# Pairwise sums of the q*k products for half of chunk 2, a norm on unscaled row sums, and a new order of all steps in a one-core transformer block

## The chip, the cores and the metric

The kernel runs on one core of one Trainium2 chip. The metric is the device time of one execution in microseconds, the median of several runs. A shorter time is better.

## What is computed

One block of a transformer on 2048 rows of 512 values in bf16: a layer norm, attention over a short dilated window, a residual sum, a second layer norm, a gated feed-forward network, and a second residual sum. Cut to what matters:

```python
H = 32; Dh = D // H; W, dil = 8, 2            # 32 heads of 16, 8 keys two rows apart
idx = pos[:, None] - arange(W) * dil           # keys s, s-2, ..., s-14
logits = einsum("bhsd,bhswd->bhsw", q, kg) * Dh ** -0.5
attn = softmax(where(mask, logits, -1e9))
o = einsum("bhsw,bhswd->bhsd", attn, vg)
h = x + o @ wo                                 # qkv = layernorm(x) @ wqkv
g = layernorm(h) @ W_gate; u = layernorm(h) @ W_up     # F = 1376
out = h + ((g * (g > 0)) * u) @ W_down
```

## The kernel before

The rows are cut into four chunks of 512 rows (0 to 3), each of four blocks of 128. Each chunk goes through the same stages.

*First norm* (`layernorm` without `residual`): statistics on VectorE (line 469), normalization on ScalarE or VectorE (lines 514, 517), transposed on TensorE (line 546) or, for chunk 3, by DMA on SP (line 535).

*q, k, v* (line 587): 12 groups of 4 matmuls of 512 columns into a PSUM bank, copied out by ScalarE (line 595). In chunk 0 the first groups are cut into pieces that wait for single slices of the weights and single blocks of x.

*Scores*: the window's 8 offsets are done in two halves of 4. For a half, VectorE multiplies q with the shifted k in two instructions of 4096 elements a partition (line 638; chunk 0 in pieces of 2048, line 653), each for two of the four channel groups. TensorE then sums over channels with a selector matrix (line 644): 16 matmuls a half, each 32 columns wide, four side by side. For the two halves of chunk 3 the tuple `PRE` makes it otherwise: VectorE first adds the two products (line 682), and 8 matmuls are left (line 689).

*Softmax and values*: exponentials on ScalarE (line 703); the sum over the window (lines 735, 720), its reciprocal (726, 729), the scaling (747); the weights are spread over partitions by DMAs on SP (line 763); VectorE multiplies with v (lines 795, 810), and the 8 products are added by an accumulating DMA from POOL (line 838) and two VectorE steps (lines 798, 832, in chunk 0 also 802).

*Output projection and residual* (line 876): TensorE, then line 887 on VectorE adds x and keeps the row sum in `sm`.

*Second norm* (`layernorm` with `residual`): line 452 scales each row sum by -1/D into `mv`, line 458 on ScalarE sums the squares of x minus mean, line 512 on VectorE subtracts the mean. The division by the deviation is left to the end of the feed-forward network, as a factor of 1/variance (lines 479, 486). The rows are transposed on TensorE for chunk 0 and by four DMAs on SP for chunks 1 to 3 (line 535).

*Feed-forward*: gate and up (line 949; the last 96 columns line 916), ScalarE copies them out (953, 956), VectorE multiplies them (977, tail 926), the tail is transposed by a DMA on SP (935), and the down projection (line 1000) follows in two parts, 8 of the 11 groups and then 3. The end is added on ScalarE and a POOL DMA (chunks 0 and 1) or on VectorE (line 1008, chunks 2 and 3), then stored.

**What sets the order.** Every step is an `Op` in a plan. The table `RANK` gives a number for each step, and `Plan.order` takes the steps in that order, works out a start for each from the durations that are written beside the steps (`MM`, `D40` and so on, and the times at which loads are expected, `XT` and `WT`), and issues them sorted by that start. On the chip each engine then runs its own list in order, with waits where data is needed. So a change of `RANK` or of a duration can move any step against any other, on every engine and on the DMA queues of SP and POOL. Buffers are shared: 8 PSUM banks, 6 big tiles of 4096 elements, two tiles each for the gate and up results.

Of the kernel before, what the change touches and what calls it, by code (L numbers as in the profile page):

```python
# [8 lines left out]
P = 128  # L9
BF16 = mybir.dt.bfloat16  # L10
F32 = mybir.dt.float32
I32 = mybir.dt.int32
ACT = mybir.ActivationFunctionType
# [80 lines left out]
class Plan:  # L94
# [21 lines left out]
    def order(self):  # L116
        self.flight = [8.65, 9.0, 9.4, 11.5, 12.9, 14.9, 16.2, 19.6]
        waiting = sorted(self.ops, key=lambda o: (o.prio, o.seq), reverse=True) if RANK else list(self.ops)
        free = {}
# [82 lines left out]
def kernel(  # L202
# [20 lines left out]
    PADL = 16  # L223
    DEN1 = (0, 1, 2, 3)
    BCD = {(0,0):"SSSS",(0,1):"SSSS",(1,0):"SSSS",(1,1):"SSSS",(2,0):"SSSS",(2,1):"SSSS",(3,0):"SSSS",(3,1):"SSSS"}
    PRE = ((3,0),(3,1))
    PRD = ()
    ODA = (0, 1)
    LATE = "ud"
# [860 lines left out]
```

## Time and profile before

| | us |
|---|---|
| median of 3 runs (lowest, highest) | 192.83 (192.31, 192.97) |
| the profiled execution | 193.22 |
| its span, first to last instruction | 191.3 |
| TensorE matmuls busy | 185.3 (97%) |
| VectorE busy | 149.6 (78%) |
| ScalarE busy | 115.2 (60%) |
| GpSimd busy | 18.5 (10%) |

The profile calls TensorE's matmuls PE and its weight loads PEld, VectorE DVE, ScalarE ACT and GpSimd POOL; a q behind an engine's name is the list of DMAs that it issues. Rows of the timeline and of the chain of waits begin with the start and the length in microseconds; in brackets stands how long the engine was idle before and what ended that. Groups give the count, the busy time and the mean length of one in ns. A VectorE instruction's length is more than the distance to the next one, since neighbours overlap a little, so a run of equal instructions gives the step. The granted TensorE clock was 0.997 over the span.

### The profile page before, as it was taken

What the parts mean: (1) busy time and instruction counts of PE and PEld (TensorE: products, weight loads), DVE (VectorE), ACT (ScalarE), POOL (GpSimd) and SP (SyncE); (2) the same over time, 40 slices, a digit from 0 to 9 for tenths busy, and PEclk for the clock granted to TensorE, in tenths of its full rate; (3) what the DMA queues carried; (4) which work ended last, traced back from release to release, by engine and by line L of the source; (5) the groups of instructions that cost most, each with busy time, mean ns of one, the idle gap of its engine ahead of it and who ended that gap; (6) DMA issues with size and microseconds to landing.
All of it is one profiled execution on the core that took longest, in us unless ns stands there. A gap on an engine that the chain in (4) does not pass through costs nothing.

```text
span 191.3 us, 3033 instructions
## 1 busy us (share of the span) xinstructions
PE 185.3 (97%) x1101; PEld 96.5 (50%) x1120; DVE 149.6 (78%) x246; ACT 115.2 (60%) x236; POOL 18.5 (10%) x34
## 2 busy tenths in 40 slices
PE   7899999999999999999999999999999999999993
PEld 7795555544455444644445544444446444445452
DVE  6899999999999999999999987999627503212632
ACT  2589999976748967753454875144855528517500
POOL 3000002500000042000055000042100000000000
PEclk9999999999999999999999999999999999999998
DMA  5998464992068589993479916779900460120302
GB/s 159 331 351 327 102 157 84 200 196 45 0 258 228 168 154 193 183 279 61 88 131 186 203 33 139 164 151 186 211 4 0 82 165 0 31 82 0 82 25 88
DMA packets 26718, 26.44 MB, mean 138 GB/s; under 512 B 12528, under 2 KB 22608, under 8 KB 26704
## 3 DMA queue, kind: packets, MB, share of 16 engines
q1 hardware_dynamic: 23248, 16.39, 30.9%
q0 software_dynamic: 2736, 8.91, 25.1%
q10 hardware_dynamic: 720, 0.95, 1.5%
q8 instruction: 9, 0.15, 0.3%
q14 instruction: 5, 0.04, 0.1%
HBM read 8.42 MB, written 2.10 MB: 55 GB/s over the span
## 4 chain that ended last, share of the span: by engine, by line
PE 94%; DMA 3%; issue 1%; ACTq 0%; DVE 0%
PE bank L949 36%; PE bank L587 22%; PE bank L1000 20%; PE bank L876 7%; DMA wqk_sb<-in_A_wqkv_dram 3%; PE bank L644 3%; PE bank L916 3%; PE bank L546 2%; PE bank L689 1%; PE bank L720 0%; ACTq L324 0%; ACTq L322 0%; DVE row L1008 0%
## 5 line engine op out<-in xcount | busy, mean ns | idle before, releaser
L949 PE MATMUL bank<-quad,wgu_sb 128*128 128x512 bf16 x311 | 72.1, 379 | 0.4
L949 PEld LDWEIGHTS <-wgu_sb 128*128 128x128 bf16 x320 | 30.9, 98 | 36.9 <-issue 1.7
L1000 PE MATMUL bank<-wd_sb,gT 128*128 128x512 bf16 (+3 forms) x195 | 39.6, 355 | 0.2
L956 ACT ACTIVATE gr<-bank 128x512 bf16<-128x512 f32 x40 | 23.2, 607 | 17.0 <-PE bank L949 13.0
L977 DVE TENSOR_TENSOR gT<-gr,up_sb 128x1024 bf16<-128x1024 bf16 x20 | 13.7, 688 | 23.5 <-ACT up_sb L953 20.3
L587 PE MATMUL bank<-quad,wqk_sb 128*128 128x512 bf16 (+2 forms) x171 | 30.0, 319 | 1.0 <-DMA wqk_sb<-in_A_wqkv_dram 0.7
L953 ACT CAST up_sb<-bank 128x512 bf16<-128x512 f32 x40 | 22.6, 594 | 10.5 <-PE bank L949 8.5
L1000 PEld LDWEIGHTS <-gT 128*128 128x128 bf16 (+1 forms) x198 | 18.5, 98 | 19.9
L638 DVE TENSOR_TENSOR big<-quad,kT 128x4096 bf16<-128x4096 bf16 x11 | 24.9, 2283 | 0.0
L587 PEld LDWEIGHTS <-wqk_sb 128*128 128x128 bf16 x176 | 16.9, 114 | 11.2 <-DMA wqk_sb<-in_A_wqkv_dram 0.9
L795 DVE TENSOR_TENSOR big<-big,vT 128x4096 bf16<-128x4096 bf16 x9 | 20.2, 2282 | 0.0
L458 ACT ACTIVATE junk<-x_sm,mv 128x512 bf16<-128x512 bf16 x16 | 11.7, 730 | 10.0 <-DVE mv L452 9.9
L587 PE MATMUL bank<-quad,wv_sb 128*128 128x512 bf16 x63 | 15.6, 379 | 0.1
L876 PE MATMUL bank<-wo_sb,quad 128*128 128x512 bf16 x63 | 15.2, 379 | 0.1
L838 POOL DMA_DIRECT2D big<-big x12 | 11.2, 1018 | 38.5 <-PE bank L587 29.4
L887 DVE SCALAR_TENSOR_TENSOR x_sm<-x_sm,bank 128x512 bf16<-128x512 bf16 x16 | 10.5, 680 | 3.7 <-PE bank L876 3.7
L798 DVE TENSOR_TENSOR big<-big 128x1024 bf16<-128x1024 bf16 (+2 forms) x18 | 11.5, 655 | 0.1
L1008 DVE SCALAR_TENSOR_TENSOR row<-bank,iv,x_sm 128x512 bf16<-128x512 f32 (+2 forms) x10 | 6.2, 640 | 6.8 <-PE bank L1000 6.8
L469 DVE BATCH_NORM_STATS2 st<-x_sm 128x6 f32<-128x512 bf16 x16 | 10.3, 681 | 1.2 <-DMA x_sm<-in_A_x_dram 1.2
L595 ACT CAST kT<-bank 128x512 bf16<-128x512 f32 x16 | 9.1, 592 | 2.8 <-DVE big L638 2.8
L595 ACT CAST quad<-bank 128x512 bf16<-128x512 f32 x16 | 9.4, 596 | 2.1 <-PE bank L587 1.9
L595 ACT CAST vT<-bank 128x512 bf16<-128x512 f32 x16 | 9.4, 596 | 2.0 <-PE bank L587 2.0
(79 smaller groups left out, 173.7 us busy)
## 6 DMA issues: line engine op xcount, KB each, us to landing
big<-big POOLq DMA_DIRECT2D x12, 512.0 KB, 5.7
big<-ex SPq DMA_DIRECT2D x32, 128.0 KB, 2.7
wqk_sb<-wqk_sb POOLq DMA_DIRECT2D x3, 512.0 KB, 4.5
wgu_sb<-in_B_W_gate_dram SPq DMA_DIRECT2D x1, 1376.0 KB, 11.2
wgu_sb<-in_B_W_up_dram SPq DMA_DIRECT2D x2, 688.0 KB, 4.7
wd_sb<-in_B_W_down_dram SPq DMA_DIRECT2D x2, 640.0 KB, 5.2
x_sm<-in_A_x_dram SPq DMA_DIRECT2D x2, 512.0 KB, 7.2
x_sm<-up_sb POOLq DMA_DIRECT2D x4, 256.0 KB, 5.1
```

What stands on the lines that cost most here:

```text
L458: nc.scalar.activation(out=junk[:, j % 2, :], in_=h.t[:] if h else x_sm[:, tk * BPC + j, :], func=ACT.Square, bias=mv.t[:, j, 0:1], scale= ...
L587: nc.tensor.matmul(mm.t[:, lo:hi], lhsT=wv_sb[:, dt, t:D:NT] if c == 2 else wqk_sb[:, dt, c * D + t:(c + 1) * D:NT], rhs=xnT.t[:, dt, lo:h ...
L595: nc.scalar.copy(out=o, in_=mm.t[:])
L638: V.tensor_tensor(out=pb.t[:].rearrange("p (t w) s -> p t w s", t=2), in0=q4, in1=k4, op=ALU.mult)
L795: V.tensor_tensor(out=mt.t[:], in0=ab.t[:], in1=v8, op=ALU.mult)
L798: V.tensor_tensor(out=mt.t[:, 0:n, :], in0=mt.t[:, 0:n, :], in1=mt.t[:, n:2 * n, :], op=ALU.add)
L876: nc.tensor.matmul(od.t[:], lhsT=OT.t[:, t, j * P:(j + 1) * P], rhs=wo_sb[:, t, :], start=(t == 0), stop=(t == NT - 1 and tk not in RPE))
L949: nc.tensor.matmul(mm.t[:fs, lo:hi], lhsT=wgu_sb[:, dt, g, ft * P: ft * P + fs], rhs=hnT.t[:, dt, lo:hi], start=(dt == 0), stop=(dt == NT ...
L953: nc.scalar.copy(out=ub.t[:fs, i, :], in_=um.t[:fs, :])
L956: nc.scalar.activation(out=gr.t[:fs, i, :], in_=gm.t[:fs, :], func=ACT.Relu)
L977: V.tensor_tensor(out=gt.t[:fs, 0:n, :], in0=gr.t[:fs, 0:n, :], in1=ub.t[:fs, 0:n, :], op=ALU.mult)
L1000: nc.tensor.matmul(od.t[:, c0:c1], lhsT=gts[ft].t[:fs, ft % 2, j * P:(j + 1) * P], rhs=wd_sb[:fs, ft, c0:c1], start=(ft == 0), stop=(ft == ...
```

## The change

Four things change.

1. `PRE` also holds (2, 1): in half 1 of chunk 2 VectorE adds the two products, and the scores take 8 matmuls instead of 16.
2. The second norm uses the row sums as they are. Line 452 is gone; the squares are taken of (sum - 512 x), the rows are written as 512 x - sum, and the epsilon is scaled by 512 squared. `eps_t` gets a second column, one more memset on POOL in the setup. The factor cancels in the 1/variance at the end.
3. Many durations of the planner are set anew: the expected loads, the DMAs' landing times and when a late transfer is assumed.
4. `RANK` is a new table.

```diff
-    PRE = ((3,0),(3,1))
+    PRE = ((2,1),(3,0),(3,1))
...
-    eps_t = sb.tile([P, 1], F32, name="eps_t")
+    eps_t = sb.tile([P, 2], F32, name="eps_t")
...
-        nc.gpsimd.memset(eps_t[:], EPS)
+        nc.gpsimd.memset(eps_t[:, 0:1], EPS)
+        nc.gpsimd.memset(eps_t[:, 1:2], EPS * D * D)
...
-    XT = (3.1, 3.25, 4.1, 5.9, 7.15, 8.65, 9.0, 9.4, 12.9, 14.85)
+    XT = (3.45, 3.65, 4.05, 5.3, 7.15, 8.65, 9.0, 9.4, 13.0, 14.5)
...
-                    late = 3.0 if at < free.get("DT", -1.0) + 0.8 else 0.0
+                    late = 3.0 if at < free.get("DT", -1.0) - 0.5 else 0.0
...
-                    def f_nm(j=j):
-                        V.tensor_scalar(out=mv.t[:, j, 0:1], in0=sm.t[:, j:j + 1], scalar1=-1.0 / D,
-                                        scalar2=None, op0=ALU.mult)
...
-                                             bias=mv.t[:, j, 0:1], scale=1.0, accum_out=sq.t[:, j:j + 1])
+                                             bias=sm.t[:, j:j + 1], scale=-float(D), accum_out=sq.t[:, j:j + 1])
...
-                    V.tensor_scalar(out=xn.t[:], in0=x, scalar1=mv.t[:, j, 0:1], scalar2=None, op0=ALU.add)
+                    V.tensor_scalar(out=xn.t[:], in0=x, scalar1=float(D), scalar2=sm.t[:, j:j + 1], op0=ALU.mult, op1=ALU.subtract)
```

The new order at three places. First VectorE between the scaling of chunk 1's softmax weights (`ex`, second row of the first piece) and the first multiplication with v. Before:

```order
L747 TENSOR_TENSOR ex_100<-ex_100,rec_103 128x512
L638 TENSOR_TENSOR big_91<-quad_87,kT 128x4096
L638 TENSOR_TENSOR big_89<-quad_87,kT 128x4096
L638 TENSOR_TENSOR big_92<-quad_87,kT 128x4096
L795 TENSOR_TENSOR wqk_sb<-big_88,vT 128x4096
L795 TENSOR_TENSOR big_90<-big_88,vT 128x4096
```

After the change (the lines have moved by a few: 638 is 635, 682 is 679, 795 is 799):

```order
L751 TENSOR_TENSOR ex_100<-ex_100,rec_103 128x512
L635 TENSOR_TENSOR big_92<-quad_87,kT 128x4096
L635 TENSOR_TENSOR big_89<-quad_87,kT 128x4096
L679 TENSOR_TENSOR big_91<-big_91,big_92 128x4096
L635 TENSOR_TENSOR big_90<-quad_87,kT 128x4096
L981 TENSOR_TENSOR gT_93<-gr_111,up_sb_110 128x1024
L799 TENSOR_TENSOR wqk_sb<-big_88,vT 128x4096
```

The sum of chunk 2's two products (L679) and one gate-up product now stand ahead of the multiplications with v of chunk 1.

Second, VectorE at the second norm of chunk 1 (`x_sm,sm_122` are the residual sums with their row sums, `row` the rows to be transposed). Before:

```order
L926 TENSOR_TENSOR row_104<-gr_111,bank_139 128x2x96
L452 TENSOR_SCALAR mv_118<-sm_122 128x1
L512 TENSOR_SCALAR row_107<-x_sm,mv_118 128x512
L926 TENSOR_TENSOR row_104<-gr_111,bank_144 128x2x96
L887 SCALAR_TENSOR_TENSOR x_sm,sm_122<-x_sm,bank_140 128x512
L452 TENSOR_SCALAR mv_118<-sm_122 128x1 x2
L512 TENSOR_SCALAR row_108<-x_sm,mv_118 128x512
L977 TENSOR_TENSOR gT_98<-gr_112,up_sb_110 128x1024
```

After (887 is 891, 512 is 509, 977 is 981):

```order
L891 SCALAR_TENSOR_TENSOR x_sm,sm_122<-x_sm,bank_142 128x512
L981 TENSOR_TENSOR gT_98<-gr_112,up_sb_110 128x1024
L509 TENSOR_SCALAR row_105<-x_sm,sm_122 128x512
L891 SCALAR_TENSOR_TENSOR x_sm,sm_122<-x_sm,bank_143 128x512
L509 TENSOR_SCALAR row_108<-x_sm,sm_122 128x512
L891 SCALAR_TENSOR_TENSOR x_sm,sm_122<-x_sm,bank_139 128x512
L509 TENSOR_SCALAR row_107<-x_sm,sm_122 128x512
```

The scaled row sums (L452) are gone, each residual sum is followed by its subtraction, and the two tail products (L926) have moved far ahead.

Third, SP's list at the same place: the transposes of chunk 1's rows (`quad_81`), of chunk 0's tail products (`gT_97`), and the DMAs that spread chunk 2's softmax weights (from `ex`). Before:

```order
L763 DMA big_88<-ex_102 128x1x512 x4
L535 DMA_TRANSPOSE quad_81<-row_107 128x4x128
L935 DMA_TRANSPOSE gT_97<-row_104 128x4x128
L535 DMA_TRANSPOSE quad_81<-row_105 128x4x128
L535 DMA_TRANSPOSE quad_81<-row_108 128x4x128
L535 DMA_TRANSPOSE quad_81<-row_106 128x4x128
```

After (535 is 532, 935 is 939, 763 is 767):

```order
L939 DMA_TRANSPOSE gT_97<-row_106 128x4x128
L532 DMA_TRANSPOSE quad_81<-row_105 128x4x128
L532 DMA_TRANSPOSE quad_81<-row_108 128x4x128
L532 DMA_TRANSPOSE quad_81<-row_107 128x4x128
L532 DMA_TRANSPOSE quad_81<-row_104 128x4x128
L767 DMA big_88<-ex_102 128x1x512 x4
```

The tail's transpose now stands ahead of the four rows' transposes, and the spreading DMAs stand behind them.

More of the change, by code (lines that the diff above doesn't have):

```diff
@@ L459, in f_sq @@
                                              func=ACT.Square,
-                                             bias=mv.t[:, j, 0:1], scale=1.0, accum_out=sq.t[:, j:j + 1])
-                    a = nms[j] = add((ln + "nm" + gk, tk), "DVE", DSM, f_nm, [src[j][0]], pr, take=[mv], use=[sm], lat=DL)
-                    ag.append(add((ln + "sq" + gk, tk), "ACT", 0.66 if h else 0.72, f_sq, [a], pr,
-                                  take=[sq], use=[mv] + ([h] if h else []), lat=AL))
+                                             bias=sm.t[:, j:j + 1], scale=-float(D), accum_out=sq.t[:, j:j + 1])
+                    ag.append(add((ln + "sq" + gk, tk), "ACT", 0.66 if h else 0.72, f_sq, [src[j][0]], pr,
+                                  take=[sq], use=[sm] + ([h] if h else []), lat=AL))
                 else:
@@ L522, in norm @@
                 f = lambda: f_xn(j, xn)
-                d, u = ([nms[j]], [mv]) if residual else ([e], [nb, rs] if on_act else [mv, rs])
+                d, u = ([src[j][0]], [sm]) if residual else ([e], [nb, rs] if on_act else [mv, rs])
                 if on_act:
                     return xn, add((ln + "xn" + gk, tk), "ACT", AX, f, d, pr, take=[xn], use=u, lat=AL)
-                return xn, add((ln + "xn" + gk, tk), "DVE", DXN, f, d, pr, take=[xn], use=u, lat=DL)
+                return xn, add((ln + "xn" + gk, tk), "DVE", 0.27 if residual else DXN, f, d, pr, take=[xn], use=u, lat=DL)
             step = 1 if tk == 0 and not residual else 2
@@ L684, with f_pb, f_sc @@
                 a = add(("pa%d" % hf, tk), "DVE", D40, f_pa, [a for a, _, _ in prd], apr, use=[b for _, b, _ in prd], lat=DL)
-                def f_sc(sc=sc, pb=prd[0][1]):
-                    for u in range(2):
+                nu = 2
+                if (tk, hf) in PRE2:
+                    def f_pb(p0=prd[0][1]):
+                        V.tensor_tensor(out=p0.t[:, 0:4, :], in0=p0.t[:, 0:4, :], in1=p0.t[:, 4:8, :], op=ALU.add)
+                    a = add(("pb%d" % hf, tk), "DVE", D20, f_pb, [a], apr, use=[prd[0][1]], lat=DL)
+                    nu = 1
+                def f_sc(sc=sc, pb=prd[0][1], nu=nu):
+                    for u in range(nu):
                         for g in range(4):
@@ L894 @@
             else:
-                a = add(("rs%d" % j, tk), "DVE", 0.63, f_rs, [a], base + 50, take=[sm], use=[od], lat=DL)
+                a = add(("rs%d" % j, tk), "DVE", 0.613, f_rs, [a], base + 50, take=[sm], use=[od], lat=DL)
             hd.append((a, od))
```

37 lines of the change are left out of this document (19 added, 18 removed), and 76 rows, old and new, of the table RANK.

## The prediction

> **What bounds the kernel now.** I read the page first: the busy line, two rows of the slices, and the chain of the work that ended last.
>
> ```profile
> span 191.3 us, 3033 instructions
> ...
> PE 185.3 (97%) x1101; PEld 96.5 (50%) x1120; DVE 149.6 (78%) x246; ACT 115.2 (60%) x236; POOL 18.5 (10%) x34
> ...
> PE   7899999999999999999999999999999999999993
> ...
> DVE  6899999999999999999999987999627503212632
> ...
> PE 94%; DMA 3%; issue 1%; ACTq 0%; DVE 0%
> ```
>
> The chain is TensorE for 94%. VectorE is as full as TensorE for the first 24 slices and half empty after them. So there are two questions: what TensorE has to do, and whether VectorE feeds it in time in the first 110 us. A busy TensorE may still wait inside a busy stretch, so I went on to the chain piece by piece (start, length, what) and to TensorE's timeline at its start.
>
> ```profile
> 8.14 0.81 PE L587 MATMUL bank<-quad,wqk_sb 128*128 128x128 bf16 x11 [0.69 <-DMA wqk_sb<-in_A_wqkv_dram]
> ```
> ```profile
> 60.58 0.98 PE bank L644 x16
> ...
> 95.38 0.55 PE bank L689 x8
> ...
> 120.66 7.13 PE bank L1000 x33
> ...
> 188.20 0.35 DVE row L1008
> ```
>
> The last wait of TensorE with a length worth naming ends at 8.14 us, when a slice of the q/k weights lands. From there to 188.2 the chain is one piece of TensorE behind the other: 33 matmuls of 512 columns take 7.13 us, 0.216 each, and the only breaks are the short pieces called issue, 1% of the span in all. So the time is: 8.1 us of loads, 180 us of matmuls without a gap, and a tail of 191.3 - 188.2 = 3.1 us (one VectorE piece of 0.35, then the last store). Whatever is taken from TensorE in those 180 us is gained whole; whatever makes it wait is lost whole, because nothing later can catch it up.
>
> **What the change takes from TensorE.** Half 1 of chunk 2 had 16 score matmuls and now has 8. Both forms stand in the chain above: 16 cost 0.98 us, 8 (chunk 3, which already had them) cost 0.55. That is **-0.43 us**. TensorE has 2242 rows in the order of before and 2226 now, 8 matmuls and their 8 weight loads less, so this is all that TensorE gains.
>
> **What it puts on VectorE.** These rows carry the prices: first the group, then the timeline.
>
> ```profile
> L682 DVE TENSOR_TENSOR big<-big,big 128x4096 bf16<-128x4096 bf16 x1 | 2.3, 2285 | 0.0
> ```
> ```profile
> 7.83 0.79 DVE L517 TENSOR_SCALAR row<-x_sm,mv,rs 128x512 bf16<-128x512 bf16 x2
> ...
> 55.47 0.32 DVE L452 TENSOR_SCALAR mv<-sm 128x1 f32<-128x1 f32 x4
> ...
> 56.05 1.13 DVE L512 TENSOR_SCALAR row<-x_sm,mv 128x512 bf16<-128x512 bf16 x4
> 57.44 6.68 DVE L638 TENSOR_TENSOR big<-quad,kT 128x4096 bf16<-128x4096 bf16 x3
> ...
> 119.45 0.15 DVE L452 TENSOR_SCALAR mv<-sm 128x1 f32<-128x1 f32 x1
> 119.64 0.35 DVE L512 TENSOR_SCALAR row<-x_sm,mv 128x512 bf16<-128x512 bf16 x1
> ```
>
> The new sum of 4096 elements is the 2285 ns instruction. Behind another it starts (6.68 - 2.28) / 2 = **2.20 us** later, so it adds 2.20. The 16 scaled row sums go: four in a row cost 0.08 each, one alone with the wait behind it 0.19 (119.45 to 119.64). That is -1.3 to -3.0 in all; I take 0.09 each, near the row of four, -1.4. The subtraction now has two operations with one value from a tile. Its price is not in the trace. From below stands L512, (1.13 - 0.35) / 3 = 0.26 a step; from above L517, two operations with two values from tiles, 0.79 - 0.40 = 0.39. I take 0.26, the row of the same place and operands, and keep 16 x 0.13 = 2.1 us for the range. VectorE's net is +0.8 us, and between -0.8 and +3.0. The squares on ScalarE keep their count and shape, and no longer wait for a row sum.
>
> All of this lies beside TensorE's work. It costs nothing as long as VectorE's results still come before TensorE wants them. That depends on the new order, so I took the places where TensorE waits for VectorE and counted, for each, what stands ahead of it now and not before, at the steps above and at these: 0.60 for a gate-up product or a 1024-element tree step, 0.27 for the small tail product, 0.34 for a 512-element product, 0.61 for a residual sum. First the margins of before: the last VectorE piece, then the matmuls that need it.
>
> ```profile
> 81.39 0.43 DVE L832 TENSOR_TENSOR quad<-big 128x512 bf16<-128x512 bf16 x1
> ...
> 113.60 1.09 DVE L832 TENSOR_TENSOR quad<-big 128x512 bf16<-128x512 bf16 x3
> ```
> ```profile
> 82.25 3.62 PE L876 MATMUL bank<-wo_sb,quad 128*128 128x512 bf16 x16
> ...
> 115.32 2.75 PE L876 MATMUL bank<-wo_sb,quad 128*128 128x512 bf16 x12
> ```
>
> - Output projection of chunk 0: one 4096 product (2.20) has moved behind it on VectorE, and on TensorE one score group (0.98) and one group of four matmuls (0.86). VectorE has 0.4 more room than before.
> - Output projection of chunk 1: VectorE done at 81.82, TensorE there at 82.25, margin 0.4. Now VectorE has +2.20 + 0.60 + 2 x 0.27 - 4 x 0.09 - 0.34 = +2.6 ahead; TensorE has two down-projection halves of 8 matmuls more and the 8 score matmuls less, 3.46 - 0.43 = +3.0. Margin 0.8.
> - Chunk 2: 114.69 against 115.32, margin 0.6. VectorE +2.20 + 0.60 + 2 x 0.34 - 8 x 0.09 - 0.27 = +2.5, TensorE again +3.0. Margin 1.1.
> - The scores of chunk 2, half 1, which wait for the new sum: VectorE +4.0 ahead, TensorE +5.9. Before, the first product of L638 above was done by 59.7 and the scores began at 60.58: 0.9 then, 2.7 now.
>
> So at these places the new order has more room than the old one, and the searched order has paid for the 2.20 us by moving TensorE's own work forward.
>
> **The one place with less room** is the first gate/up matmul of chunk 1, which needs four transposes on SP, each issued behind a normalized row. Before (SP's own times, the landing times of the four, and TensorE):
>
> ```profile
> 87.23 1.78 SPq L535 DMA_TRANSPOSE quad<-row  x1
> 89.11 1.20 SPq L935 DMA_TRANSPOSE gT<-row  x1
> 90.41 3.87 SPq L535 DMA_TRANSPOSE quad<-row  x3
> ```
> ```profile
> DMA to landing us min/median/max: 2.4/2.5/3.0
> ```
> ```profile
> 95.86 8.81 PE L949 MATMUL bank<-quad,wgu_sb 128*128 128x512 bf16 x39
> ```
>
> Five transposes went one behind the other; the last was issued 1.2 before 94.28, at 93.07, and landed 2.4 later, at 95.5: margin 0.4. Now the first row is ready later by 2.20 + 0.27 + 0.60 - 5 x 0.09 - 0.34 - 2 x 0.61 = 1.06. The transpose of the tail product (L935) has gone ahead of the four, because its product is made some 12 us earlier, and that saves 1.30. TensorE is there 0.43 earlier. Margin 0.4 - 1.06 + 1.30 - 0.43 = 0.2: I count no wait, and this is the tightest place of the new order.
>
> **The start.** The loads are issued as before, but one more memset on POOL stands ahead of the one that guards the last weight slice, and TensorE uses that slice after four matmuls fewer (2 x 0.11 = 0.22 us earlier).
>
> ```profile
> 3.74 0.33 SPq L339 DMA_DIRECT2D wqk_sb<-in_A_wqkv_dram  x1
> ```
> ```profile
> wqk_sb<-in_A_wqkv_dram SPq DMA_DIRECT2D x1, 256.0 KB, 5.7
> ```
>
> It landed at 9.44; TensorE wanted it at about 9.7 and now wants it at 9.5. I put 0.05 for that, between 0 and 0.2. The statistics of the fourth block of x now stand ahead of the second block's normalization, which ties two more steps to that load; in this execution the matmuls of the first two slices, which wait till 8.14 anyway, cover it.
>
> **Sum**: -0.43 + 0.05 = -0.38. The profiled execution took 193.22 us (191.3 and 1.9 around it), so it would take 192.84. The median of the runs shown is 192.83, 0.39 lower; by the same step it comes to **192.45 us**.
>
> [...]
>
> **Rivals.**
> 1. *The start gains more.* The steady part of this execution has no gap to remove, yet the runs shown go from 192.31 to 193.22. That spread must come from loads at the start, the tail, or waits that this execution did not have. If the new order is less sensitive to them by 0.3 us, the median is 192.1. For: a whole group of four q matmuls now stands among the pieces that wait for the last slices and rows. Against: the first slices set 8.14 in either order. 0.27.
> 2. *The transposes of chunk 1 come late* and TensorE waits at its first gate/up matmul. It costs from 0.2 us of lateness on, and the kernel is slower beyond my bound of 0.3% from 0.2 + 0.4 + 0.6 = 1.2. If all four transposes went like the first one (1.78 each, landing in 3.0), they would be 3 x 0.53 + 0.6 = 2.2 late, 2.0 lost: 192.45 + 2.0 = 194.4. For: margin 0.2, and the subtraction at 0.39 would take 4 x 0.13 of it. Against: three of the four rows showed 1.25. 0.16.
> 3. *VectorE is the bound*: it is full for 110 us, so its net of +0.8 is the change, 192.83 + 0.8 = 193.6. Against it: TensorE has no gap in those 110 us that a faster VectorE could close, and the margins above. 0.03. [...]
> 4. *The change does not do what it says*: the removed score matmuls cost nothing where they stand now. Then 192.8. Against: 16 and 8 differ by 0.43 in two stages of the same chain. 0.04.
>
> **Chances.** My forecast 0.50. Within 0.3% (0.58 us, about what a measurement of this kernel can tell from no change) lie nearly all of the forecast's own spread, rival 4 and half-late transposes: 0.52. Faster: rival 1 and a little of the forecast, 0.29. Slower: rivals 2 and 3, 0.19. The range goes from 191.9 (rival 1 with some to spare) to 193.4 (a wait of 1 us), and leaves out the rest of rival 2 and rival 3.
>
> **What would show it.** Eight matmuls fewer in the score line of chunk 2 and a piece of 0.55 in the chain; VectorE busy some 0.8 longer; no wait of TensorE after 8.2 us; margins at the output projections as listed; the last of chunk 1's transposes landing near 95.2. A gap of TensorE before the new kernel's first gate/up matmul of chunk 1 (its line 953), or before an output projection (its line 880), would make the prediction wrong, and so would a start other than 8.1.

## The result and the profile after

The changed kernel took **194.24 us** in the median of 22 runs (192.68 to 197.09), the kernel before 192.94 in 22 runs beside them (192.18 to 193.50). The ratio is 1.0059, 95% interval 1.0037 to 1.0081: slower, where 192.45 was forecast, and outside the range of 191.9 to 193.4. (The ratio leaves out the two slowest runs, 196.80 and 197.09, which are more than 1.5% above the fastest.) The spread has grown more than the median: the lower third of the runs lies at 192.7 to 193.4, inside the range of the kernel before, and the upper third at 194.7 to 197.1.

From the page of the changed kernel: the span, the busy times, two rows of the slices (a digit is the busy share of a fortieth of the span, in tenths), and the clock that TensorE was granted.

```profile
span 193.2 us, 3034 instructions
...
PE 186.9 (97%) x1112; PEld 97.2 (50%) x1112; DVE 151.1 (78%) x231; ACT 116.5 (60%) x236; POOL 18.5 (10%) x35
...
PE   7599999999999999999999999999999999999993
...
PEclk9879999999999999999999999999999999999999
```

TensorE is busy 1.6 us longer although it has 8 matmuls less, and the clock row has a dip in the second and third slice that the kernel before does not have. Both belong to the start. A piece of the chain of waits, then VectorE's and TensorE's timelines there:

```profile
1.70 5.69 DMA x_sm<-in_A_x_dram
```
```profile
5.60 0.38 DVE L514 TENSOR_SCALAR row<-x_sm,mv,rs 128x512 bf16<-128x512 bf16 x1
7.41 0.69 DVE L466 BATCH_NORM_STATS2 st<-x_sm 128x6 f32<-128x512 bf16 x1 [1.43 <-DMA x_sm<-in_A_x_dram]
8.02 0.40 DVE L514 TENSOR_SCALAR row<-x_sm,mv,rs 128x512 bf16<-128x512 bf16 x1
```
```profile
6.27 0.61 PE L435 MATMUL bank<-warm 128*128 128x128 bf16 x8
8.47 0.61 PE L543 MATMUL bank<-identity,row 128*128 128x128 bf16 x4 [1.59 <-DVE row L514]
8.87 0.63 PE L584 MATMUL bank<-quad,wqk_sb 128*128 128x128 bf16 x4
```

The statistics of the fourth block of x (L466) wait until 7.41 for that block to land. Behind them in VectorE's list stands the normalization of the second block (L514), at 8.02, though that block has long been there. TensorE's second transposes follow at 8.47, and until then it is idle for 1.59 us. In the kernel before, whose fourth block landed at 6.65, the second block was normalized ahead of those statistics:

```profile
5.72 0.70 DVE L517 TENSOR_SCALAR row<-x_sm,mv,rs 128x512 bf16<-128x512 bf16 x2
6.69 0.69 DVE L469 BATCH_NORM_STATS2 st<-x_sm 128x6 f32<-128x512 bf16 x1 [0.27 <-DMA x_sm<-in_A_x_dram]
```

After the wait, TensorE runs on half its clock: 0.50 was granted from 8.48 to 11.90 us, and 1.00 before and behind. Busy times of the changed kernel in three stretches (length, TensorE, its weight loads, VectorE, ScalarE, GpSimd, the granted clock, DMA share, GB/s):

```profile
5.06:8.48 3.42, 1.45 (x23) 1.11 (x21) 1.99 (x8) 1.84 (x7) 0.00 (x0) 1.00 0.92 318
8.48:11.90 3.42, 3.42 (x30) 3.23 (x31) 3.10 (x9) 1.67 (x4) 0.00 (x0) 0.50 0.94 255
11.90:15.30 3.40, 3.40 (x44) 2.98 (x43) 1.99 (x6) 1.83 (x5) 0.00 (x0) 1.00 1.09 376
```

3.42 us at a clock of 0.50 are 1.7 us of TensorE's work lost, an estimate from these two numbers. In the stretch of the same length just before, 5.06 to 8.48, TensorE was busy for 1.45 us of 3.42.

The steady part did what was forecast of it. Two pieces of the chain:

```profile
68.44 0.55 PE bank L693 x8
...
96.96 0.54 PE bank L693 x8
97.51 2.70 PE bank L953 x12
```

Chunk 2's half takes 8 matmuls and 0.55, and at chunk 1's first gate/up matmul, the tightest place, TensorE goes on without a gap. So in this execution the 0.43 was gained, and the start with its half clock lost some 2 us (the span is 1.9 longer).

### The profile page after: what moved, and what is told of

Same layout as the page of the kernel before. It is cut to its first block, busy times and chain, and to the rows that moved or that the text cites. A ratio compares the mean times of both kernels' runs of the same rounds, so it can differ in the third digit from the quotient of the medians.

```text
span 193.2 us, 3034 instructions
## 1 busy us (share of the span) xinstructions
PE 186.9 (97%) x1112; PEld 97.2 (50%) x1112; DVE 151.1 (78%) x231; ACT 116.5 (60%) x236; POOL 18.5 (10%) x35
## 4 chain that ended last, share of the span: by engine, by line
PE 94%; DMA 3%; issue 0%; SPq 0%; DVE 0%
PE bank L953 36%; PE bank L584 22%; PE bank L1004 20%; PE bank L880 7%; DMA x_sm<-in_A_x_dram 3%; PE bank L920 3%; PE bank L641 3%; PE bank L543 2%; PE bank L693 1%; PE bank L724 0%; SPq L323 0%; DVE row L514 0%; DVE row L1012 0%; DVE st L466 0%
## 5 line engine op out<-in xcount | busy, mean ns | idle before, releaser
L584 PE MATMUL bank<-quad,wqk_sb 128*128 128x512 bf16 (+2 forms) x176 | 31.2, 331 | 0.0
L584 PEld LDWEIGHTS <-wqk_sb 128*128 128x128 bf16 x176 | 17.7, 117 | 10.7 <-issue 0.8
L799 DVE TENSOR_TENSOR big<-big,vT 128x4096 bf16<-128x4096 bf16 x10 | 22.4, 2281 | 0.0
L456 ACT ACTIVATE junk<-x_sm,sm 128x512 bf16<-128x512 bf16 x16 | 11.7, 732 | 8.7 <-DVE x_sm L891 8.6
L802 DVE TENSOR_TENSOR big<-big 128x1024 bf16<-128x1024 bf16 (+2 forms) x19 | 12.1, 659 | 1.9 <-DMA big<-big 1.7
L891 DVE SCALAR_TENSOR_TENSOR x_sm<-x_sm,bank 128x512 bf16<-128x512 bf16 x16 | 10.8, 681 | 1.4 <-PE bank L880 1.4
L466 DVE BATCH_NORM_STATS2 st<-x_sm 128x6 f32<-128x512 bf16 x16 | 10.2, 678 | 1.7 <-DMA x_sm<-in_A_x_dram 1.7
L650 DVE TENSOR_TENSOR big<-quad,kT 128x2048 bf16<-128x2048 bf16 x8 | 9.3, 1219 | 1.4 <-ACT quad L592 1.4
```

Of the source, the lines that this page charges most:

```text
L456: nc.scalar.activation(out=junk[:, j % 2, :], in_=h.t[:] if h else x_sm[:, tk * BPC + j, :], func=ACT.Square, bias=sm.t[:, j:j + 1], scale ...
L584: nc.tensor.matmul(mm.t[:, lo:hi], lhsT=wv_sb[:, dt, t:D:NT] if c == 2 else wqk_sb[:, dt, c * D + t:(c + 1) * D:NT], rhs=xnT.t[:, dt, lo:h ...
L799: V.tensor_tensor(out=mt.t[:], in0=ab.t[:], in1=v8, op=ALU.mult)
L802: V.tensor_tensor(out=mt.t[:, 0:n, :], in0=mt.t[:, 0:n, :], in1=mt.t[:, n:2 * n, :], op=ALU.add)
```

## The experiments

Each ran in one set with the kernel before, and the ratio is to that kernel. Sets on different chips are compared by their ratios. Theory A: only the start costs. Theory B: the steady part loses the time. The later theories are named where they came up.

### The start taken apart

The first four: the order of two steps exchanged in either kernel, more filling matmuls, and the changed kernel once more.

```diff
+RANK[31], RANK[42] = RANK[42], RANK[31]        # second block's normalization <-> fourth block's statistics
```
```diff
-    NWARM, NFILL = 46, (8, 0, 0)
+    NWARM, NFILL = 46, (24, 0, 0)
```

*Changed kernel, second block first:*

> The changed kernel with one exchange on VectorE at the start: the second block of x is normalized before the statistics of the fourth block, as in the kernel before; every other list of instructions is the same. Theory A (the start: the second block's transposes wait for the fourth block's load, TensorE idles some 1.7 us and its clock falls to half for one stretch of 3.4 us): the median falls to 192.3 to 192.7, all runs within about 0.7 us of it, first matmul of the weights back near 8.1, no half clock behind it. Theory B (the steady part: VectorE's added sum makes transposes or sums late in most executions, and the start is a second, smaller cost): the median stays at 193.6 or above and the runs still spread by 2 us and more.

193.24 (192.04 to 194.62), ratio 1.0023 [0.9995, 1.0050]. Not the 192.3 to 192.7 of theory A. The unchanged kernel took 193.24 in the same set (below), so the exchange gained nothing that these runs can tell. TensorE shows why:

```profile
7.05 0.42 PE L584 MATMUL bank<-quad,wqk_sb 128*128 128x128 bf16 x4
8.07 0.40 PE L543 MATMUL bank<-identity,row 128*128 128x128 bf16 x4 [0.59 <-DVE row L514]
```

Its second transposes now come at 6.66, but the wait has moved to the third block's row, which still stands behind the fourth block's statistics.

*Changed kernel, 24 filling matmuls:*

> The changed kernel with 24 instead of 8 small idle-time matmuls behind the first transposes, 0.9 us more of work for TensorE in the time in which it waits for the second block; the wait itself is kept. Theory A, if the half clock is the larger part: the median falls by 0.6 to 1.2 us to about 193.0 to 193.6, since the wait of 0.3 to 0.5 stays but the clock holds in more runs. Theory A, if the wait is the larger part, and theory B: no change from 194.2.

193.30 (192.55 to 194.21), ratio 1.0014 [0.9995, 1.0032]. The fourth block landed at 8.13 in its profile and the second transposes came at 9.20, 1.31 us idle, with the clock at 1.00 throughout:

```profile
9.20 0.40 PE L543 MATMUL bank<-identity,row 128*128 128x128 bf16 x4 [1.31 <-DVE row L514]
```

The median is no better than that of the unchanged kernel in the same set; what differs is the clock. All 12 runs had a mean clock of 0.997 or more; of the 22 runs of the changed kernel, four had 0.989 to 0.991, among them three of the four slowest.

*Kernel before, fourth block first:*

> The kernel before with the mirrored exchange alone: the statistics of the fourth block of x stand ahead of the second block's normalization. Theory A: slower by 1.0 to 1.7 us, 194 to 194.6, with a spread of 3 us or more, as the changed kernel shows plus its 0.4. Theory B: within 0.3 us of the kernel before.

193.37 (192.90 to 197.77), ratio 1.0026 [1.0004, 1.0047]. Slower, by less than expected: the fourth block landed early in its profile (6.57), and before's list has more matmuls ahead of the third block. Even so the q/k matmuls ran from 8.31 in place of 8.14:

```profile
7.63 0.40 PE L546 MATMUL bank<-identity,row 128*128 128x128 bf16 x4 [1.16 <-DVE row L517]
...
8.31 0.83 PE L587 MATMUL bank<-quad,wqk_sb 128*128 128x128 bf16 x12
```

This is the plainest test of the step, with nothing else changed: it costs 0.26%, and the one run of 197.77 had a mean clock of 0.983.

*The changed kernel again, in the set of these experiments:*

> The changed kernel as it is, on the same chip as the others. Both theories: 193.6 to 194.8 in the median, 192.7 to 197 over the runs. Its profile tells more: theory A expects TensorE's stretches without a gap again from the first weight matmuls to the end, with a late start or a half clock; theory B expects a gap of TensorE between 60 and 180 us.

193.24 (192.60 to 195.83), ratio 1.0013 [0.9985, 1.0041]. Here it is within 0.3%. The fourth block's statistics began at 7.31, the second transposes at 8.37, and no half clock followed. Between the two sets of the same kernel lie 1.0 us in the median (ratios 1.0059 and 1.0013); the landing of the loads may make this difference, but no run separates it from the chip.

### A load made late, and the start untied

```diff
-                        (nc.sync, "x", 3), (nc.scalar, "w", 2), (nc.sync, "x", BPC)):
+                        (nc.sync, "x", BPC), (nc.scalar, "w", 2), (nc.sync, "x", 3)):
```

> The new kernel, with the load of the fourth block of x issued behind that of the fifth block on SP's queue, so that it lands later (estimate from the 0.5 to 0.7 us between landings on that queue: 0.5 to 1.0 later). Theory A: the second block's normalization and transposes come later by as much, and the time rises nearly one to one: 193.7 to 194.6 in place of 193.2, some executions with a stretch of half clock behind the wait. Theory B: the load has room at the start, 193.2 as the unchanged new kernel.

194.62 (193.29 to 198.32), ratio 1.0087 [1.0052, 1.0123]. The profiled run, the slowest of the set, has a late start and a half clock behind it (a granted clock of 0.97 over 10 to 60 us, and of 1.00 in the 10 us before):

```profile
9.14 0.40 PE L543 MATMUL bank<-identity,row 128*128 128x128 bf16 x4 [2.00 <-DVE row L514]
```

> The same later load of the fourth block of x in the kernel before. Theory A: only the eviction of the second transposes and the third block stand behind that load there, and its matmuls have till 8.14 anyway, so it loses less than the new kernel does: 193.0 to 193.4, ratio 1.000 to 1.002. Theory B: no difference between the two kernels in this, both keep their time.

193.58 (193.37 to 194.36), ratio 1.0052 [1.0034, 1.0069]. The same late load costs the changed kernel 0.74% over its ratio of 1.0013, and the kernel before 0.52%, with a spread of 1.0 us against 5.0. Both are clear of no change, so in either kernel the start hangs on that load; the two costs are not told apart, and the kernel before was expected at 1.002 at most. Its profile shows why it loses too: VectorE's eviction of the second transposes stands behind the fourth block there as well:

```profile
8.53 0.27 PE L587 MATMUL bank<-quad,wqk_sb 128*128 128x128 bf16 x2 [0.73 <-DVE quad L560]
```

Then two ways to give the changed kernel a better start: the fourth block's steps moved behind those of the first three (19 entries of `RANK`), and the first 52 steps in the order of the kernel before.

> The new kernel, with the statistics and the aggregate of the fourth block of x moved behind the normalization of the second and of the third block and behind the eviction on VectorE, and that block's logarithm and exponential on ScalarE moved behind the eviction of the third block; all else in the order of the new kernel. Theory A (the start: what is made from the second and the third block stands behind the load of the fourth): nothing of the first three blocks waits for that load any more, TensorE's last wait at the start ends at 8.1 to 8.4 in the profile, and the time is that of the kernel before less the 0.43 of the score matmuls: 192.3 to 192.8, ratio 0.997 to 0.999. Theory B (the steady part loses it: the longer VectorE list): the time stays that of the unchanged new kernel on this chip, 193.2 to 194.2, and TensorE has gaps after 10 us.

194.78 (193.40 to 195.65), ratio 1.0096 [1.0068, 1.0125]. Worse than the unchanged kernel, which neither theory expected. In the profile the wait moved on to the fourth block's own row, which is wanted soon after:

```profile
9.37 0.40 PE L546 MATMUL bank<-identity,row 128*128 128x128 bf16 x4 [1.11 <-DVE row L517]
```

> The new kernel, in which the first 52 steps (the loads, the four statistics and normalizations, the first transposes and the first q/k matmuls) stand in the order of the kernel before; everything behind them in the order of the new kernel. Theory A: the start is that of the kernel before, the rest is the new kernel's: 192.96 - 0.43 = 192.5, ratio 0.9978, and the spread of the runs as narrow as that of the kernel before (1.9 us of span). Theory B: 193.2 to 194.2, as the unchanged new kernel.

193.50 (192.51 to 195.29), ratio 1.0043 [1.0015, 1.0070]. **Here theory A alone fell.** The start is cured: TensorE is busy 8.73 of the first 10 us, 8.22 in the kernel before and 7.03 in the changed one. The profiled run took 192.76, near the forecast, but seven of the 12 took over 193.4. So theory B has a part in it. The profile has a wait that the slow start had covered. SP's list and TensorE at the first gate/up matmul of chunk 1:

```profile
87.90 5.99 SPq L535 DMA_TRANSPOSE quad<-row  x4
```
```profile
94.24 0.61 PE L696 MATMUL bank<-big,sel 128*32 128x512 bf16 x8
95.26 2.10 PE L956 MATMUL bank<-quad,wgu_sb 128*128 128x512 bf16 x9 [0.41 <-issue]
```

TensorE waits 0.41, which the profile puts to no engine; the last of the four transposes was issued at 92.67, and the fastest of them landed 2.4 after its issue, so it is the transposes of chunk 1 that it waits for, the place where the prediction had counted a margin of 0.2.

### Who is late at chunk 1's transposes

Theory C: VectorE's longer list. Theory D: chunk 2's spreading DMAs collide with the accumulating DMAs of chunk 0's output. All with the start of before:

```diff
-    PRE = ((2,1),(3,0),(3,1))
+    PRE = ((3,0),(3,1))
```

> The new kernel with the start of the kernel before, and without the addition of the pair in half 1 of chunk 2 (16 score matmuls there again, no sum of 4096 elements on VectorE); the new second norm and the rest of the new order stay. Theory C (VectorE: its longer list makes chunk 1's normalized rows and their transposes late, and TensorE waits at the first gate/up matmul of chunk 1, 0.45 us in the profile with the start of before): VectorE comes there 2.2 us earlier, the wait goes, the score matmuls cost their 0.43 again, and the spread shrinks to that of the kernel before: 192.8 to 193.1. Theory D (late broadcasts of chunk 2, which share the transfers' time with the accumulating transfers of chunk 0's output): the addition is not the cause, the time rises by 0.43 over the same kernel with the addition: 193.9. Theory A (only the start cost): 192.9, and then the kernel with the addition and this start should have been 192.5, which it was not.

194.85 (193.95 to 195.69), ratio 1.0092 [1.0058, 1.0125]. All three expectations missed. The wait at chunk 1 is gone (TensorE from 95.45 to 96.00 without a gap), and yet the kernel is slower by 0.49% than with the addition (ratio 1.0043), 0.9 us, where the 8 matmuls account for 0.43. The profile puts it at the very end, where a store of output rows holds SP's list for 1.54 us in place of 0.33; in that stretch runs one transfer of the queue that brings instructions (packets, MB, share):

```profile
187.56 1.54 SPq L1018 DMA_DIRECT2D out_dram<-row  x1
```
```profile
q8 instruction: 1, 0.02, 4.2%
```

The last row lands 3.20 us behind the last matmul in place of 2.01.

> The new kernel with the start of the kernel before, without the two accumulating transfers that add chunk 0's feed-forward output to the residual stream (that addition is left out of the output). Theory D: chunk 2's broadcasts land 2.5 to 3 us after their issue in place of up to 5, VectorE's wait of 1.0 for them goes, and with it the slow executions: 192.5 to 193.0 with a narrow spread. Theory C: TensorE still waits at the first gate/up matmul of chunk 1 for the transposes, which these transfers do not stand ahead of: 193.3 to 193.6.

193.23 (192.34 to 195.69), ratio 1.0010 [0.9981, 1.0040]. The spread stays (3.4 us), so D is not the cause of it, though the wait at chunk 1 is not in this profile.

> The new kernel with the start of the kernel before, and the 512-element product of chunk 2's weights that stands ahead of the last of chunk 1's four normalized rows on VectorE moved behind that row: the last transpose is issued 0.34 earlier. Theory C: the wait of TensorE at the first gate/up matmul of chunk 1 falls from 0.45 to about 0.1, and the median by about 0.3 against the same kernel without this exchange: 193.2. Theory D: no change, 193.5.

193.30 (192.50 to 195.02), ratio 1.0020 [0.9993, 1.0046]. The median moved as C has it (its ratio of 1.0020 is not told apart from 1.0043), but the profile says otherwise: the wait was 0.50, not 0.1, since the second of the four transposes held SP for 2.17 us:

```profile
95.41 3.40 PE L953 MATMUL bank<-quad,wgu_sb 128*128 128x512 bf16 x15 [0.50 <-issue]
```

In the profile with the start of before it held it for 2.08, and in the one without the addition for 1.21:

```profile
89.20 2.08 SPq L535 DMA_TRANSPOSE quad<-row  x1
```
```profile
89.97 1.21 SPq L532 DMA_TRANSPOSE quad<-row  x1
```

*Theory F*: TensorE's instructions come in transfers of 16384 bytes (queue 8 of the profile; that they are TensorE's is read from how they move with its instructions), and an issue on SP that falls into one can be held until it is in. The times of that queue's packets in the traces, us:

```
                                 fifth fetch     transposes held       ninth fetch      last stores    last matmul
                                                 (1.2 otherwise)                        held           to landing
before                           87.32- 88.57    first, 1.78           186.06-187.02    third, 0.97    1.86
after                            91.37- 92.30    second, 1.51          none             none           2.01
after again                      89.78- 90.73    second, 1.58          none             none           2.01
start of before                  88.82- 90.21    second, 2.08          none             none           2.00
same, row first                  88.87- 90.35    second, 2.17          none             none           2.00
same, no pair added              87.23- 88.19    none                  187.04-188.73    third, 1.54    3.20
```

A held transpose ends 0.4 to 1.1 us behind the end of the fetch, a held store 0.36. Not every issue in a fetch is held: in four other profiles the first of the four transposes was issued inside one and took 1.22 to 1.29. And a hold is not yet a wait of TensorE. A wait at chunk 1's gate/up matmul stands in five profiles (0.14 to 0.68), each with a transpose held for 1.8 to 2.3 us; where it took 1.5 to 1.7, none is over 0.1. The changed kernel has 16 TensorE instructions fewer (8 matmuls and 8 weight loads), so by F every fetch comes 16 instructions later in the program. The ninth then falls off the end, and the fifth falls onto the second transpose of chunk 1. The kernel without the addition has them back, and its ninth falls onto the third of the last stores, with three more behind it on SP's list.

### The fetch moved, and nothing else

```diff
-    NWARM, NFILL = 46, (8, 0, 0)
+    NWARM, NFILL = 46, (16, 0, 0)        # in the kernel without the addition: (0, 0, 0)
```

> The new kernel with 16 filling matmuls behind the first block's transposes in place of 8; 8 matmuls and 8 weight loads more on TensorE, in a stretch in which it waits over 1 us for the fourth block of x anyway. Theory F (TensorE's instructions come in blocks of 16 KB; while one is fetched, an issue on SP is held until it is in): the eight instruction pairs move every fetch ahead by 16 instructions: a ninth fetch falls on the last output stores again, 1 to 1.5 us before TensorE's last matmul, and holds one of them: 1.0 to 1.3 us slower than the unchanged new kernel (193.24 and 194.24 in its two sets of runs): 194.3 to 195.3. The kernel with 24 filling matmuls, whose ninth fetch came 2.9 us before the end, took 193.30. Theory C (VectorE alone) and theory A (the start alone): as the unchanged kernel, 193.2 to 194.2, and no more than with 24.

194.25 (193.60 to 194.65), ratio 1.0075 [1.0048, 1.0102], just under the 194.3 expected. It is clear of the 1.0014 with 24 filling matmuls and of the 1.0013 with 8, but not of the 1.0059 that the first set had with 8. The profile is plainer: the store that was free is held, the transpose that was held is free, and the last row lands 2.91 us behind the last matmul in place of 2.01:

```profile
187.28 1.24 SPq L1018 DMA_DIRECT2D out_dram<-row  x1
```
```profile
q8 instruction: 1, 0.02, 3.4%
```

> The kernel of the new order with the start of before and without the addition of the pair (194.85), now without the 8 filling matmuls: TensorE has as many instructions as the new kernel again. Theory F: no fetch on the last stores, the end comes 2.0 us behind the last matmul again in place of 3.2: 193.4 to 193.8. Theory C or A: nothing changes, 194.85; and should the filling matmuls have kept the clock up, it would be slower than that.

193.75 (192.77 to 194.60), ratio 1.0048 [1.0020, 1.0076]: 1.1 us less than with the 8 filling matmuls (the ratios differ by 0.44%, 0.85 us, with intervals that overlap a little), by leaving out filling at the start. The same store:

```profile
187.66 0.33 SPq L1018 DMA_DIRECT2D out_dram<-row  x1
```

The last row lands 2.00 us behind the last matmul in place of 3.20. So F holds both ways: 16 TensorE instructions at the start move the end by 0.9 and 1.2 us in the profiles.

### The change in parts, and a better version

The new norm alone in the order of before; the same with 16 filling matmuls; the same with the addition put into the old order; and two controls.

> The new second norm alone (no scaled row sums, two operations in the subtraction) in the order of the kernel before; no addition of the pair. VectorE has 16 small instructions less. Theory C: VectorE has more room than in the kernel before and TensorE the same work: 192.7 to 193.0, spread as before or narrower. If the new form of the norm itself cost time (a longer subtraction, squares that come at another time), it would be 193.1 to 193.6.

192.77 (192.09 to 193.56), ratio 0.9972 [0.9946, 0.9999].

> The new second norm and the addition of the pair in the order of the kernel before; only the addition is put in behind the second product, and the two score groups of chunk 2 go behind three and two groups of gate/up matmuls. Theory C (VectorE's list ahead of chunk 1's normalized rows decides): VectorE comes to those rows some 1.3 to 1.7 later than in the norm-only kernel (2.20 less the scaled row sums that are gone), TensorE waits at the first gate/up matmul of chunk 1 for 0.7 to 1.3, and the saved 0.43 is more than lost: 192.77 - 0.43 + 1.0 = 193.3, between 193.0 and 193.7. If the order that the search made is what costs the time, and not the addition: 192.3 to 192.5.

194.40 (194.03 to 194.78), ratio 1.0089 [1.0061, 1.0117]. Against the norm alone the addition costs 1.6 us there by the medians and 2.3 by the ratios, more than expected: TensorE waits at three places,

```profile
60.50 3.61 PE L953 MATMUL bank<-quad,wgu_sb 128*128 128x512 bf16 x15 [0.77 <-ACT quad L559]
73.03 0.39 PE L724 MATMUL bank<-row,same 128*128 128x512 bf16 x1 [0.28 <-DVE row L739]
83.18 3.63 PE L880 MATMUL bank<-wo_sb,quad 128*128 128x512 bf16 x16 [0.43 <-ACT gr L960]
```

The second waits for VectorE, and so does the third, as its weight loads show:

```profile
83.17 0.76 PEld L880 LDWEIGHTS <-quad 128*128 128x128 bf16 x5 [0.92 <-DVE quad L836]
```

The first waits for a copy on ScalarE, which was busy without a break for over 2 us before. Theory C fits the old order.

> The norm-only kernel (192.77) with 16 filling matmuls in place of 8, which moves the ninth fetch some 1.7 us ahead of where it held the third of the last stores for 1.78. Theory F: the end comes 1.9 instead of 2.1 us behind the last matmul, at most 0.2 gained if the 0.45 of filling is hidden by the wait for the weights: 192.6 to 192.8; a wider price of the filling at the start would show as up to 193.1.

**192.47** (192.32 to 192.88), ratio 0.9976 [0.9956, 0.9996]: the lowest median, with a spread of 0.56 us; by the ratio it is not told apart from the 0.9972 with 8 filling matmuls. No store is held, and the last row lands 1.87 behind the last matmul (2.10 with 8 filling matmuls).

> The kernel before with 16 filling matmuls in place of 8. Theory F: the fetch at the end moves from 186.1 to some 184.4, ahead of the last stores, and the hold of the third of them (0.97 to 1.6 us in its profiles) goes; the transposes of chunk 1 are not held. That gains 0 to 0.3: 192.6 to 193.0, with a spread narrower than 1.9 us. If the norm is what made the other kernel fast, it stays at 192.8 to 193.0; if the moved fetch and the filling did, it comes to 192.5.

192.72 (192.41 to 193.10), ratio 0.9987 [0.9964, 1.0011], spread 0.69 in place of the 2.4 of the kernel before beside it. So the narrow spread comes with the filling, and what is left for the norm, 0.25 us, is not told apart from nothing. The filling also moves the fetches, and these runs do not separate the two.

> The new kernel with the start of the kernel before (193.50) and 24 filling matmuls in place of 8: the fetches come 32 TensorE instructions earlier. Theory F: the transposes of chunk 1 are issued 1.2 us apart, none held, the wait of 0.45 at the first gate/up matmul is gone or under 0.2, and no store at the end is held. The filling costs 0.9 us more of TensorE at a place where it may have 0 to 0.5 of room. 192.5 to 193.0 if the filling is hidden, up to 193.4 if it is not. Theory C (VectorE's list alone, whatever the fetch): the wait at the first gate/up matmul stays at 0.4, unless TensorE comes later by the filling.

193.09 (192.92 to 193.69), ratio 1.0015 [1.0000, 1.0030]. With both causes gone the spread is 0.8 and no transpose of chunk 1 is held, nor a store for more than 0.2 us. TensorE's wait at chunk 1 is gone too:

```profile
95.62 1.68 PE L953 MATMUL bank<-quad,wgu_sb 128*128 128x512 bf16 x7
```

Yet the 0.43 does not come out. The filling ends at 8.23 and the first q/k matmul starts at 8.07, where it started at 7.43 with 8: 0.6 us of it is paid. The version without that price was not found.

## Why the prediction was wrong

**The step that failed is the start**, put at 0.05 us, between 0 and 0.2. The prediction saw that two more steps are tied to the load of the fourth block and let them cost nothing, "in this execution the matmuls of the first two slices, which wait till 8.14 anyway, cover it". That took one landing, 6.65, for the rule. With the load in its old place the fourth block's statistics began at 6.80 to 8.13 in five profiles with the changed start, and at 6.22 to 7.38 in twelve with the start of before; whether the new order itself makes the load later was not tested. The second transposes stand 1.06 us behind that, and the first q/k matmuls follow at 8.61 (changed kernel again), 8.87 (first profile) and 9.4 (24 filling matmuls): 0.5 to 1.3 later than 8.14. The cover was a draw as well: with the start of before the q/k matmuls ran from 7.43 with no wait for the weights.

In some executions a half clock also followed the idle time, another 1.5 us (the first profile of the changed kernel against the one taken again, from the second transposes to the end: 184.7 and 183.2). The two profiles with a half clock had TensorE busy for 1.45 and 1.42 of the 3.41 us before it, the length of the stretch at 0.50 in the first (the second is the changed kernel with the late load); in the other eighteen none of the first three stretches of this length, counted from where the full clock begins, had less than 1.95.

That the step costs is shown: 0.26% where it alone was put into the kernel before. That it makes the whole of the 0.59% is not. Undoing it for the second block alone gained nothing that the runs can tell, and with the start of before the ratio was still 1.0043, for the reasons below and for one that is open. The prediction had named a start other than 8.1 as a sign of being wrong, and that came true.

The other steps:

- **8 score matmuls less, -0.43**: right as work: the piece of the chain is 0.55 long, as forecast. Two profiles without half clock, each with 19 matmul rows missing, show TensorE 185.33 us busy before and 184.96 in the changed kernel (again), 0.37 less; between kernels of equal work such sums differ by more than that (186.57 for the norm alone). Little of it reaches the time: with the start of before and as many fetches, the kernel with the addition (1.0043) and the one without (1.0048) are not told apart.
- **VectorE +0.8**: it is 1.4 longer busy (149.63 to 151.07). The addition is as priced (2.28). The subtraction with two operations costs what the old one did: 348 ns the mean of 16 in both. The norm alone takes 1.6 off VectorE in the old order (148.05), near the 1.4 counted. In the new order it takes 0.7 (148.93 without the addition). There each subtraction stands behind the residual sum that it waits for, and these two groups are busy 5.4 and 10.8 us, against 4.9 and 10.5 with the norm alone.
- **Margins at the output projections**: no wait there in either profile of the changed kernel, right.
- **Margin 0.2 at chunk 1's transposes**: the place was right, the size not. It is used up by a hold that the prediction had seen in the row of before (1.78 for the first transpose) and kept at that place; it belongs to the fetch, not to the transpose. It cost nothing in the two profiles of the changed kernel and 0.14 to 0.68 in five others.
- **What was not in the sum**: the end. The new order issues the last stores so that the last row lands 2.01 behind the last matmul in place of 1.86, 0.15 more. And TensorE waits 0.15 to 0.17 at the first gate/up matmul of chunk 2 (from 128.02 in the changed kernel again, by the distance of the starts, 0.36 to 0.39 in place of 0.216).

These terms give, for the changed kernel again: -0.37 for the matmuls, +0.54 for the first 10 us (7.68 busy in place of 8.22), +0.15 for the end, +0.17 at chunk 2: +0.5, where its span is 0.25 longer (191.56 against 191.31). They add up to twice what the span shows, so they fit in size only.

The rivals: *the start gains more* had the right term and the wrong sign. *Transposes late* is there with a third of its price at most (0.68 of 2.0). *VectorE is the bound* got a chance of 0.03; for the addition in the old order it comes near the truth (+1.6, with TensorE waiting at three places), in the new order no such waits stand in the profiles.

**What stays open.** The kernel with the start of before has runs of 193 us span at full clock, and no profile fell on one; which wait makes them is not shown. And some runs of the new order have up to 1.3 us more between the span and the time than the usual 1.8. In one profile the ninth fetch came at 197.34, behind the end of the span at 195.6, and that run lay 2.72 above its span. The runs go with it. Of the kernels whose profile has nine fetches in the span, none of 229 runs lay more than 2.01 above its span. Of those with eight, 30 of 106 did, ten of them among the 22 of the changed kernel (2.04 to 2.90); this leaves aside the twelve without the accumulating DMAs, which all lay 2.08 to 2.45 above. So the longer time outside the span was seen with kernels whose profile has no ninth fetch in the span, and once with that fetch behind its end; what makes it longer, no run shows.

## What to carry to other kernels

A wait that one profile shows as covered is covered for that draw of the loads only (here the fourth block's statistics began at 6.80 to 8.13 us in five profiles): read the same landing in several executions before a step tied to it is costed at nothing, and keep steps of data that is there ahead of the ones that wait (the exchange alone cost 0.26%). Where an engine is full, count instructions as well as time: here 16 instructions more or fewer at the start put a fetch of code onto the last stores or took it off them, and a store that met one cost 0.9 to 1.2 us in the profiles, where 8 score matmuls less were counted at 0.43. Parts of a searched order that are put back one at a time can be slower than either whole: here the ratio without the addition was 1.0092, against 1.0043 with it and 1 for the kernel before.

## What the runs showed of the hardware

**Issues on SP that met a fetch of TensorE's instructions took up to 1.4 us longer, but not all of them.** The packets of queue 8 have 16384 bytes and take 0.88 to 1.69 us; the kernel before has 9 of them in its span and the changed one 8. In 11 profiles a transpose of chunk 1 that meets one takes 1.5 to 2.3 us in place of 1.2, and in six the third of the last stores takes 0.97 to 1.77 in place of 0.33. Not every issue is held. The first transpose went out inside a fetch in four profiles and took 1.22 to 1.29 (one at 87.41 in 86.67 to 87.79, kernel before with the fourth block first). The first or second of these stores was not held inside a fetch: one at 186.87 in a fetch of 186.22 to 187.39 (changed kernel, 24 filling matmuls), one at 185.14 in 184.47 to 185.83 (kernel before, 16). Which issue in a fetch is held, and why, no run shows. TensorE's matmuls have no gap of over 0.02 us at the eight fetches of the changed kernel. A held store cost 0.9 to 1.2 us at the end of a kernel.

**A half clock came after stretches in which TensorE was busy for less than half.** It was busy for 1.45 and 1.42 us of 3.41 in the two profiles with a half clock; in another, with 1.95, the clock stayed at full. With 16 or 24 of the small filling matmuls in place of 8 no run of 54 had a mean clock under 0.995. The spread of before's order fell with 16 from 2.4 to 0.7 us, but they move the fetches too.
